# Turning gathered token rows by DMA transposes instead of TensorE for three pairs of tiles, and moving two small steps a place later

## The chip, the cores and the metric

One Trainium2 chip, of which one core runs the program. The metric is the device time of one execution in microseconds, lower is better.

## The reference

A gated linear attention recurrence, whose output rows are the tokens of a mixture of experts with two experts for each token.

```python
B, H, S, D = (4, 8, 768, 48)
for t in range(S):
    state = alpha[:, :, t, :, None] * state + einsum('bhd,bhe->bhde', k[:, :, t], v[:, :, t])
    y[:, :, t] = einsum('bhd,bhde->bhe', q[:, :, t], state)
x = y.transpose(0, 2, 1, 3).reshape(3072, 384)
...
logits = x @ w_gate                                  # 8 experts
noisy_logits = logits + log1p(exp(x @ w_noise)) * noise
top2, top2_w = the two largest of each row, and their softmax
for e in range(8):
    h = maximum(x[mask] @ w1[e], 0.0)                # w1: 384 x 1024
    out[mask] += top2_w[mask, k, None] * (h @ w2[e]) # w2: 1024 x 384
```

All of it is in float32. (`log1p(exp(z))` is computed on the chip as an exponential and then a logarithm with 1 added to its input.)

## The kernel before

The kernel has two stages. The order of the instructions on each engine is written out by hand, and each engine works through its own in that order.

**The recurrence** goes over 24 chunks of 128 tokens, n = 0 to 23; six chunks are a batch and also a unit (u = 0 to 3) of the router. A chunk is a list of pieces in a fixed order: 0 loads, 1 keys, 2 inverses, 3 alphas, 4 turn_y, 5 turn_k, 6 scaled, 7 queries, 8 block, 9 output, 10 no_more, 11 state, 12 scores, 13 masked, 14 products. Within these, a piece works for a chunk further on or further back: `scores` and `masked` are those of chunk n + 1, `turn_y` is that of n - 1. TensorE (PE) turns the inputs (`tp`, L343), multiplies scores (L423), turns the keys (L450), forms the output (y, L491 and L252) and turns it into rows with the router's logits (L275); VectorE (DVE) runs two scans over the chunk (L371, L383), scales the queries (L411) and masks the scores (L443); ScalarE (ACT) copies from PSUM.

The router's work for a unit is a generator, `routing`, of nine or ten steps: the exponential (L719), the logarithm (L687), the first sums, the search for the two largest of two columns (L733, L734), of two more, then of the last two together with the exponential of the gates (L751), the counts on DVE (L757 to L781), the rank on PE (L786, L787), the table entries, and for unit 1 a check of the lists. The exponential and the logarithm need different tables of ACT, so a table load stands ahead of each switch. For units 0 and 1, `ROUTE` says behind which piece of which chunk a step goes: a pair (c, place) is chunk c + 5 of unit 0 and chunk c + 11 of unit 1. For units 2 and 3, the steps have planned times in the second stage.

**The experts** work on 24 pairs of tiles of 128 tokens, i = 0 to 23, counted from 0 here as in the code, so the fourth to the seventh pair are i = 3 to 6. Pairs 0 to 7 take the first 256 tokens of each expert, each with new weights; from pair 8 on, two pairs share the weights of an expert. The matrix products follow a scheme that saves multiplications with sums of blocks on DVE. Each step of a pair has a planned time 20 i + t. All steps of all pairs, of some small tiles and of the router's units 2 and 3 are sorted by their planned times, and that is the order of their instructions on each engine. (20 units of this plan take about 19.6 us in the first pairs.) For unit 3 the exponential and the logarithm are planned at 49.8.

What brings the rows of x of a pair to PE:
- `load_tab` reads 256 entries of the table (SP's queue for the pairs 0, 1 and 5 to 8, POOL's for the others), `find_rows` computes row numbers on DVE, and `gather` fetches the rows from DRAM into `x_in` by two indirect DMAs on POOL (L988). A row lies there as two planes of 16 bits, the low and the high halves of its 384 words.
- By TensorE (pairs 0 to 6): `joined_rows` copies the planes on ACT into whole words in `x_whole` (L286, two copies of 128 x 768 halves); `turn_x` turns 3 blocks of 128 x 128 for each of the two tiles on PE (L1191, the product into a PSUM bank of `tp`); `turned_x` copies each of the two banks into `xts` on ACT (L1195). For the pairs 3 to 6 (`in_turn`) the joins are planned at -13.9, the turns at -7.9 and -3.25 and the copies at -7.0 and -2.4.
- By the DMA (from pair 7 on): `turn_x` issues two DMA transposes of 128 x 768 halves on SP's queue (L1187), from `x_in` into `x_turned`, which is the same memory as `x_whole`; `turned_x` puts the halves together with two copies on ACT (L1198). Pair 7 has the transposes planned at -20.5, and the copies at -10.0 and -8.5.

`scaled` (L1352) is ACT's copy of a bank of the second product times the gate, `added` and `added_to_both` (L1356, L1360) add a bank to it on DVE, `relu` is L1342, and L1323, L1331 and L1338 are the products. Bank A (`o_ps`) is written by a product, scaled by ACT, and written again.

`out_of_range` tests in two parts whether a fast form of the recurrence was in range: part 0 is five small steps on DVE, planned at 117.4, part 1 a product with ones on PE (L525) and two small steps on DVE (L526, L527).

Of the kernel before, what the change touches and what calls it, by code (L numbers as in the profile page):

```python
# [19 lines left out]
def kernel(  # L20
# [35 lines left out]
    E, _, F = moe_w1.shape  # L56
# [228 lines left out]
    def whole(to, planes, copy):  # L285
        copy(out=to.bitcast(U16).rearrange("p (c w) -> p w c", w=2), in_=planes.rearrange("p (w c) -> p w c", w=2))  # L286
# [5 lines left out]
    def fast_gla(on):  # L292
# [210 lines left out]

        ROUTE = (((1, 9), (2, 8), (2, 13), (3, 4), (3, 11), (4, 8), (4, 10), (5, 4), (5, 7)), ((1, 9), (1, 12), (2, 4), (2, 8), (2, 11), (3, 8), (3, 10), (4, 4), (4, 7), (4, 12)))
        routes = [routing(u, on) for u in range(NU)]

        def route(n, place):
            for u in range(2):  # L510
                for _ in range(ROUTE[u].count((n - (u + 1) * UC + 1, place))):
                    next(routes[u], None)
# [579 lines left out]
    order_of = list(range(E)) + [E - 1 - g for g in range(E) for b in range(2)]  # L1092
    rounds = [0] * E + [1, 2] * E
    PLANNED = E + 2 * AFTER_GROUP[0]
    DEEP, BY_DMA = E - 1, E - 1
    is_new = [i < E or (i % 2 == 0 and order_of[i] != order_of[i - 1]) for i in range(NPAIR)]
    assert len(order_of) == NPAIR

# [1 line left out]
    def pairs(on):  # L1100
# [75 lines left out]
                get_x(x_in[:, s], wheres[i][:, s, 0:1], 2 if i < E else NU)  # L1176

        def joined_rows(i):
            if i >= BY_DMA:
                return  # L1180
            for s in range(2):
                whole(x_whole[:, s], x_in[:, s], nc.scalar.copy if i else nc.vector.tensor_copy)

        def turn_x(i, some=range(2)):
            for s in some:
                if i >= BY_DMA:
                    nc.sync.dma_start_transpose(out=x_turned[:, s].rearrange("p w a t -> p (w a) t"), in_=x_in[:, s])  # L1187
                    continue
                x_ps = bank["x", s] = on["tp"].tile([C, KO, C], F32, tag="tp", name="x_ps")
                for a in range(KO):  # L1190
                    nc.tensor.transpose(x_ps[:, a, :], x_whole[:, s, ds(a * C, C)], ident)  # L1191

        def turned_x(i, part):
            if i < BY_DMA:
                nc.scalar.copy(xts[i % 2][:, part], bank["x", part])  # L1195
                return
            halves = xts[i % 2].rearrange("p s a t -> p (s a t)").bitcast(U16).rearrange("p (s x w) -> p w s x", s=2, w=2)
            nc.scalar.copy(halves[:, part], x_turned[:, :, part].rearrange("p s a t -> p s (a t)"))  # L1198

        def rows_x(i):  # L1200
            return lambda a, t: xts[i % 2][:, t, a, :]
# [178 lines left out]
        T = 20.0  # L1380
        FIRST_BEHIND = 2
# [105 lines left out]
        def steps(i):  # L1487
            w = lambda f, a: w1_(i, f, a)
            v = lambda f, d: w2_(i, f, d)
            x = rows_x(i)  # L1490
            apart = i < FIRST_BEHIND
            full = i < E
            early = {0: EARLY_0, 1: EARLY_1, FIRST_BEHIND + 1: {"tab": T * i - 40.0, "find": T * i - 33.0, "gather": T * i - 32.5}, E - 1: {"tab": T * E - 57.5, "find": T * E - 52.3, "gather": T * E - 52.2},
                     E: {"tab": T * E - 33.0, "find": T * E - 25.0, "gather": T * E - 24.8, "turn": T * E - 21.8, "turned": T * E - 9.5, "joined": T * E - 8.0}}.get(i, {})
            at = lambda name, t: early.get(name, T * i + t) - T * i
            in_turn = FIRST_BEHIND < i < BY_DMA
            if full and i >= BY_DMA:
                gets = {"tab": -32.0, "find": -27.0, "gather": -26.0, "join": -22.0, "turn": -20.5, "turned": -10.0, "joined": -8.5, "sum_x": -0.5, "sum_xs": 0.3}
            elif in_turn:
                gets = {"tab": -32.0, "find": -27.0, "gather": -26.0, "join": -13.9, "turned": -7.0, "joined": -2.4, "sum_x": -0.5, "sum_xs": 0.3}  # L1500
            elif full:
                gets = {"tab": -32.0, "find": -27.0, "gather": -26.0, "join": -15.0, "turn": -11.9, "turned": -11.0,
                        "joined": -11.0, "sum_x": -7.9 if apart else -10.38, "sum_xs": -7.9 if apart else 0.3}
            else:
                gets = {"tab": -50.5, "find": -32.5 if i % 2 else -39.4, "gather": -29.5, "join": -31.0, "turn": -23.5, "turned": -12.4, "joined": -11.2,
                        "sum_x": -6.4, "sum_xs": 0.3}
            when = lambda name: at(name, gets[name])
            turns = [(-7.9, lambda: turn_x(i, (0,))), (-3.25, lambda: turn_x(i, (1,)))] if in_turn else [(when("turn"), lambda: turn_x(i))]
            w1_at = (-20.0, -17.0, -14.0 if i >= DEEP else -3.5) if i > FIRST_BEHIND else [at("w1", -29.5) + part * every.get(("w1", i), 3.0) for part in range(KO)]
            w2_at = (5.5, 8.2, 10.9, 13.6) if i > FIRST_BEHIND else [at("w2", -19.8) + part * every.get(("w2", i), 3.0) for part in range(FO // 2)]  # L1510
            loads = [(t, lambda w=w, part=part: load_part(w, i, part)) for w, ts in (("w1", w1_at), ("w2", w2_at)) for part, t in enumerate(ts)]
            s_at = (-16.5, -15.8, -7.4, -7.5) if apart else (-12.0, -11.3, -9.5, -8.8)
            t_at = (-5.2, -2.5, 0.1, 4.4) if i == 0 else (20.4, 24.6, 27.5, 24.7) if i > E else (14.5, 24.0, 27.5, 25.0)
            last = i == NPAIR - 1
            second_layer = (parted if i == 0 else last_ending if last else mixed)(i, v)
            return [(T * i + t, go) for t, go in loads] + [(T * i + t, go) for t, go in (
                (when("tab"), lambda: load_tab(i)), (when("find"), lambda: find_rows(i)), (when("gather"), lambda: gather(i)),
                (when("join"), lambda: joined_rows(i)), *turns,
                (when("turned"), lambda: turned_x(i, 0)), (when("joined"), lambda: turned_x(i, 1)),
                *([(t, lambda k=k: sum_x_deep(i, k)) for k, t in enumerate((-7.5, -7.4, -5.2, 4.5, 8.6) if i <= E else (-9.0, -8.0, -5.2, 4.5, 8.6))] if i >= DEEP else  # L1520
                  [(when("sum_x"), lambda: sum_x(i, True)), (when("sum_xs"), lambda: sum_x(i, False))]),
                *([(t, lambda k=k: sum_w1_deep(i, k)) for k, t in enumerate((-9.5, -7.0, -0.9, 0.05, 2.5, 6.0, 8.0, 10.9))] if i >= DEEP else
                  [(at(f"s{k}", t), lambda k=k: sum_w1(i, k)) for k, t in enumerate(s_at)]),
                *[(at(f"t{k}", t), lambda k=k: sum_w2(i, k)) for k, t in enumerate(t_at)],
                *(deeper(i, x) if i >= DEEP else (alone if apart else between)(i, w, x)), *second_layer)]
# [159 lines left out]
    with ExitStack() as es:  # L1685
# [5 lines left out]
        pair_steps, clear_pairs, T, latest = pairs(on)  # L1691
# [3 lines left out]
        def beside():  # L1695

            at = (-0.95, 4.75, 3.66, 6.15, 6.9, 28.5)
            left = [(at[0], lambda: put_y(LAST - 2)), (at[1], lambda: output(LAST)), (at[2], lambda: turn_y(LAST - 1)),
                    (at[3], lambda: turn_y(LAST)), (at[4], lambda: put_y(LAST - 1)), (at[5], lambda: put_y(LAST)),
                    (5 * T + 17.4, lambda: out_of_range(0)), (5 * T + 18.7, lambda: out_of_range(1))]  # L1700
            r1, r2, r3 = (6.2, 12.2, 15.2)
            when = lambda *steps: [d * T + t for d, t in steps]
            left += [(t, lambda: route_on(2)) for t in when(*((0, 17.4), (0, 17.4), (0, 18.7), (1, r1), (2, 3.5), (2, r1), (2, 9.7), (2, r2), (2, r3)))]
            left += [(t, lambda: route_on(3)) for t in when(*((2, 9.8), (2, 9.8), (3, r1), (3, r1), (3, r2), (3, r3), (4, r1), (4, r2), (4, r3)))]
            left += [(t, lambda: route_on(3)) for t in when(*[(8, 10.7), (9, 1.6), (9, 8.7), (9, 10.7), (10, 10.7), (10, 12.2), (10, 13.2), (11, 1.6)])]
            puts = when((2, 17.3), (2, 18.6), *[(3, t) for t in (3.9, 5.2, 10.1, 11.4, 12.7, 17.3, 18.6)],
                        (4, 3.9), (4, 5.2), (4, 11.4), (4, 17.3), (4, 18.6), *[(5, t) for t in (3.9, 5.2, 10.1, 11.4, 12.7, 17.3, 18.6)],
                        (6, 2.6), (6, 3.9), (6, 5.2))
            left += [(t, lambda: put_some(1, latest["sum"])) for t in puts]
            assert len(puts) == 4 * UC  # L1710
            return left
# [156 lines left out]
```

## Time and profile before

| | |
|---|---|
| time before, median of 3 runs | 632.79 us (632.18 to 632.89) |
| the profiled execution | 634.14 us, span 632.5 us |
| TensorE (PE), busy | 613.7 us |
| VectorE (DVE) | 512.2 us |
| ScalarE (ACT) | 330.4 us |
| GpSimd (POOL) | 323.2 us |
| mean granted TensorE clock | 0.995 |

The profile is of one execution, and its times are microseconds from the first instruction on. The span reaches from the first instruction to the last; what lies around it belongs to the execution's own time. "Busy" leaves out waits, and a busy PE is not PE at its peak, since matmuls are pipelined. A wait is put down to the engine and instruction that ended it.

### The profile page before, as it was taken

The numbers are of one execution on the slowest core, as the hardware profiler recorded it, in microseconds if no ns is written. First come the engines' busy times: TensorE is split into PE (matmuls) and PEld (weight loads), VectorE is DVE, ScalarE is ACT, GpSimd is POOL, SyncE is SP. The second block draws the span as 40 slices with busy tenths as digits, with TensorE's granted clock in tenths as the row PEclk, the third lists the DMA queues.
The fourth block names the chain that finished last, engine by engine and source line by source line (L and its number), as shares of the span: only waits on it lengthen the run. The fifth ranks groups of instructions, "written<-read, shape, count | busy, mean of one in ns | idle before, by whom it ended". The sixth has DMA issues, their size and how long they took to land.

```text
span 632.5 us, 14445 instructions
## 1 busy us (share of the span) xinstructions
PE 613.7 (97%) x5326; PEld 589.3 (93%) x5326; DVE 512.2 (81%) x1175; ACT 330.4 (52%) x664; POOL 323.2 (51%) x362
## 2 busy tenths in 40 slices
PE   8999999999999999999999999999999999999993
PEld 5899989988999999999999999999999999989893
DVE  8788998878759877578999999787987879878671
ACT  5778777675555453342555454545545545454340
POOL 7353277854051877775545465532655427443353
PEclk9999999999999999999999999999999999999997
DMA  9999999984862666785746776866869578775223
GB/s 144 167 199 214 219 201 170 226 160 112 264 194 100 205 199 182 205 248 98 176 103 134 176 242 135 225 149 154 260 161 234 123 181 226 178 213 134 63 40 53
DMA packets 178288, 108.56 MB, mean 172 GB/s; under 512 B 142600, under 2 KB 167667, under 8 KB 178209
## 3 DMA queue, kind: packets, MB, share of 16 engines
q1 hardware_dynamic: 137040, 33.59, 31.1%
q10 hardware_dynamic: 25840, 53.48, 27.7%
q0 software_dynamic: 15328, 20.47, 14.5%
q8 instruction: 44, 0.72, 0.5%
q14 instruction: 36, 0.29, 0.1%
HBM read 85.85 MB, written 24.22 MB: 174 GB/s over the span
## 4 chain that ended last, share of the span: by engine, by line
PE 75%; DVE 12%; issue 3%; DMA 3%; POOL 2%; ACT 2%; SPq 0%; POOLq 0%; DVEq 0%; ACTq 0%
PE h_ps L1338 14%; PE sc L1331 13%; PE o_ps L1338 11%; PE sc L1323 7%; PE c_ps L1331 6%; PE tp L343 5%; PE sc L423 4%; PE y L252 4%; PE h_ps L275 3%; PE y L491 3%; DVE wt L1204 1%; PE o_ps L465 1%; PE tp L450 1%; PE c_ps L1323 1%; DVE h L1207 1%
## 5 line engine op out<-in xcount | busy, mean ns | idle before, releaser
L972 POOL DMA_INDIRECT out_dram<-o,where x46 | 48.5, 1055 | 150.4 <-DVE o L1356 70.4
L1342 ACT ACTIVATE h<-h 128x512 f32<-128x512 f32 x89 | 55.2, 628 | 84.4 <-DVE h L1204 51.6
L988 POOL DMA_INDIRECT x_in<-x_rows,where x48 | 59.6, 1242 | 53.9 <-DVE where L1172 29.5
L980 POOL DMA_INDIRECT out_dram<-o,where x44 | 74.7, 1697 | 13.4 <-issue 13.4
L1338 PE MATMUL o_ps<-wt,hx 128*128 128x192 f32 x384 | 70.7, 327 | 0.0
L1338 PEld LDWEIGHTS o_ps<-wt,hx 128*128 128x128 f32 x384 | 61.5, 190 | 1.8 <-issue 1.8
L172 POOL DMA_INDIRECT table<-entry,place_u x48 | 53.1, 1106 | 13.9 <-issue 10.9
L1331 PE MATMUL sc<-yT,ws 128*128 128x128 f32 x408 | 56.5, 275 | 0.0
L1331 PEld LDWEIGHTS sc<-yT,ws 128*128 128x128 f32 x408 | 53.5, 191 | 0.0
L401 POOL TENSOR_TENSOR k_P<-k_P,over 128x512 f32<-128x512 f32 (+1 forms) x24 | 27.7, 1155 | 44.6 <-DVE over L383 31.5
L343 PE MATMUL tp<-ident,ins 128*128 128x128 f32 x288 | 42.0, 280 | 2.2 <-ACT k_P L393 0.7
L1352 ACT ACTIVATE o<-h_ps,tab 128x192 f32<-128x192 f32 x46 | 19.3, 420 | 40.9 <-PE h_ps L1338 33.7
L343 PEld LDWEIGHTS tp<-ident,ins 128*128 128x128 f32 x288 | 31.8, 142 | 7.2 <-ACT k_P L393 1.1
L443 DVE COPY_PREDICATED shared<-upto,sc 128x512 f32<-128x512 uint32 x47 | 31.9, 732 | 6.9 <-PE sc L423 6.4
L1338 PE MATMUL h_ps<-w,hx 128*128 128x192 f32 x192 | 35.6, 327 | 0.3 <-issue 0.3
L1338 PE MATMUL h_ps<-wt,h 128*128 128x192 f32 x192 | 35.3, 327 | 0.3 <-DVE wt L1204 0.3
L1338 PE MATMUL o_ps<-w,h 128*128 128x192 f32 x192 | 35.3, 327 | 0.2 <-DVE o L1360 0.2
L1338 PE MATMUL h_ps<-wt,hx 128*128 128x192 f32 x192 | 35.2, 326 | 0.0
L1338 PE MATMUL h_ps<-w,h 128*128 128x192 f32 x192 | 35.1, 326 | 0.0
L1198 ACT COPY xt<-x_turned 128x768 uint16<-128x768 uint16 x34 | 33.6, 1053 | 0.8 <-DMA x_turned<-x_in 0.8
L1338 PEld LDWEIGHTS h_ps<-w,hx 128*128 128x128 f32 x192 | 31.7, 190 | 0.7 <-issue 0.7
L1338 PEld LDWEIGHTS h_ps<-w,h 128*128 128x128 f32 x192 | 31.8, 190 | 0.0
(322 smaller groups left out, 1642.1 us busy)
## 6 DMA issues: line engine op xcount, KB each, us to landing
w<-in_moe_w_dram ACTq DMA_DIRECT2D x42, 512.0 KB
w<-in_moe_w_dram ACTq DMA_DIRECT2D x56, 384.0 KB
ins<-in_alpha_dram SPq DMA_DIRECT2D x24, 192.0 KB
ins<-in_k_dram SPq DMA_DIRECT2D x24, 192.0 KB
ins<-in_q_dram SPq DMA_DIRECT2D x24, 192.0 KB
vt<-in_v_dram SPq DMA_DIRECT2D x24, 192.0 KB
x_rows<-y_sb SPq DMA_DIRECT2D x24, 192.0 KB
ins<-in_moe_w_dram ACTq DMA_DIRECT2D x9, 512.0 KB
```

The lines of the kernel that those rows point to most:

```text
L172: put = nc.gpsimd.indirect_dma_start(out=table, out_offset=bass.IndirectOffsetOnAxis(ap=place, axis=0), in_=entry, in_offset=None, bounds_ ...
L343: nc.tensor.transpose(tp[:, j, :], src[:, 2 * j:2 * j + 2, :], ident)
L401: (nc.vector if n == NT - 1 else nc.gpsimd).tensor_tensor(c["k"][:, at], c["k"][:, at], over[:, at, 1:CB], op=ALU.mult)
L443: nc.vector.copy_predicated(MTs[n % 2][:, i], mask_upto, sc)
L972: put = nc.gpsimd.indirect_dma_start(out=out, out_offset=bass.IndirectOffsetOnAxis(ap=at, axis=0), in_=rows, in_offset=None, bounds_check= ...
L980: add = nc.gpsimd.indirect_dma_start(out=out, out_offset=bass.IndirectOffsetOnAxis(ap=at, axis=0), in_=rows, in_offset=None, bounds_check= ...
L988: nc.gpsimd.indirect_dma_start(out=rows, out_offset=None, in_=x_rows[0:units * UT, :], in_offset=bass.IndirectOffsetOnAxis(ap=at, axis=0), ...
L1198: nc.scalar.copy(halves[:, part], x_turned[:, :, part].rearrange("p s a t -> p s (a t)"))
L1323: nc.tensor.matmul(bank[name][:, f, :], W[:, ds(f * C, C)], X, start=new and f == 0, stop=True, skip_group_check=True)
L1331: nc.tensor.matmul(bank[name][:, 2 * h + f, :], W[h][:, ds(f * C, C)], X[h], start=new and not h and not f, stop=True, skip_group_check=True)
L1338: nc.tensor.matmul(bank[name], H[:, f, :], W[:, f, :], start=new and f == 0, stop=True, skip_group_check=True)
L1342: nc.scalar.activation(t, t if src is None else src, AF.Relu)
```

## The change

The pairs that PE turns are now 0, 1, 2 and 6, so the pairs 3, 4 and 5 take the way by the DMA, with its planned times: transposes at -20.5, copies at -10.0 and -8.5 (that is 39.5, 50.0 and 51.5 for pair 3), and no join.

In `ROUTE`, unit 1's second step, the logarithm, moves from (1, 12) to (2, 8); its third to fifth steps (the first sums and two searches) move from (2, 4), (2, 8) and (2, 11) to (2, 11), (2, 13) and (3, 4); the others stay.

The second part of the range test moves from a planned time of 118.7 to 127.0.

```diff
-        ROUTE = (((1, 9), (2, 8), (2, 13), (3, 4), (3, 11), (4, 8), (4, 10), (5, 4), (5, 7)), ((1, 9), (1, 12), (2, 4), (2, 8), (2, 11), (3, 8), (3, 10), (4, 4), (4, 7), (4, 12)))
+        ROUTE = (((1, 9), (2, 8), (2, 13), (3, 4), (3, 11), (4, 8), (4, 10), (5, 4), (5, 7)), ((1, 9), (2, 8), (2, 11), (2, 13), (3, 4), (3, 8), (3, 10), (4, 4), (4, 7), (4, 12)))
...
-    DEEP, BY_DMA = E - 1, E - 1
+    DEEP, BY_TENSOR = E - 1, (0, 1, 2, E - 2)
...
         def joined_rows(i):
-            if i >= BY_DMA:
+            if i not in BY_TENSOR:
                 return
...
         def turn_x(i, some=range(2)):
             for s in some:
-                if i >= BY_DMA:
+                if i not in BY_TENSOR:
                     nc.sync.dma_start_transpose(out=x_turned[:, s].rearrange("p w a t -> p (w a) t"), in_=x_in[:, s])
                     continue
...
         def turned_x(i, part):
-            if i < BY_DMA:
+            if i in BY_TENSOR:
                 nc.scalar.copy(xts[i % 2][:, part], bank["x", part])
                 return
...
-            in_turn = FIRST_BEHIND < i < BY_DMA
-            if full and i >= BY_DMA:
+            in_turn = FIRST_BEHIND < i and i in BY_TENSOR
+            if full and i not in BY_TENSOR:
                 gets = {"tab": -32.0, "find": -27.0, "gather": -26.0, "join": -22.0, "turn": -20.5, "turned": -10.0, "joined": -8.5, "sum_x": -0.5, "sum_xs": 0.3}
...
-                    (5 * T + 17.4, lambda: out_of_range(0)), (5 * T + 18.7, lambda: out_of_range(1))]
+                    (5 * T + 17.4, lambda: out_of_range(0)), (6 * T + 7.0, lambda: out_of_range(1))]
```

## Rows read from the trace of the kernel before

**Rows 1.** The page, part 1: busy time, share of the span, instructions.
```profile
PE 613.7 (97%) x5326; PEld 589.3 (93%) x5326; DVE 512.2 (81%) x1175; ACT 330.4 (52%) x664; POOL 323.2 (51%) x362
```

**Rows 2.** PE's waits: who waited for whom, us in total, times, longest.
```profile
PE tp L450 <- ACT noisy L687: 1.4, 1, 1.4
```

**Rows 3.** Timeline near the range test: start, us, engine, line, operation, [idle before, releaser].
```profile
268.59 0.69 DVE L1207 TENSOR_TENSOR h<-c_ps,m 128x512 f32<-128x512 f32 x1 [5.03 <-PE x_ps L1191]
269.33 1.05 PE L1323 MATMUL sc<-xt,w 128*128 128x128 f32 x8
...
271.22 0.38 PE L525 MATMUL count<-out_of,ones 128*128 128x3 f32 x2 [0.84 <-DVE out_of L536]
```

**Rows 4.** The chain that ended last, near pair 3: start, us, what.
```profile
203.93 0.61 DVE h L1207
...
204.58 2.05 PE sc L1323 x16
...
207.94 0.33 PE x_ps L1191 x3
...
209.56 1.78 PE sc L1323 x16
```

**Rows 5.** Timeline, unit 1's logarithm, ACT and PE's weight loads.
```profile
92.45 1.28 ACT L687 ACT_TABLE_LOAD   x1
...
94.71 0.42 PEld L450 LDWEIGHTS tp<-ident,k_P 128*128 128x128 f32 x4 [1.53 <-issue]
```

**Rows 6.** Timeline, chunks 13 and 14, and two rows of chunk 20.
```profile
98.10 1.16 PE L423 MATMUL sc<-q_P,k_P 48*128 48x128 f32 x16
...
99.15 0.16 DVE L733 MAX8 top<-noisy 128x8 f32<-128x8 f32 x1
...
99.84 1.34 DVE L443 COPY_PREDICATED shared<-upto,sc 128x512 f32<-128x512 uint32 x2
...
105.17 0.17 DVE L745 TENSOR_TENSOR entry<-top 128x12 f32<-128x12 f32 x1
105.37 0.23 ACT L751 ACTIVATE entry<-entry 128x12 f32<-128x12 f32 x1 [0.84 <-DVE entry L745]
...
107.41 0.44 PE L787 MATMUL h_ps<-past,ones 128*128 128x48 f32 x2
...
142.78 1.16 PE L423 MATMUL sc<-q_P,k_P 48*128 48x128 f32 x16
...
143.97 1.36 DVE L443 COPY_PREDICATED shared<-upto,sc 128x512 f32<-128x512 uint32 x2 [0.62 <-PE sc L423]
```

**Rows 7.** Timeline, pairs 8 and 9: gather, DMA transposes, ACT's copies behind them.
```profile
291.29 1.05 POOL L988 DMA_INDIRECT x_in<-x_rows,where  x1 [6.08 <-DVE where L1172]
...
294.46 2.94 SPq L1187 DMA_TRANSPOSE x_turned<-x_in  x2
...
302.05 1.07 ACT L1198 COPY xt<-x_turned 128x768 uint16<-128x768 uint16 x1 [0.78 <-DMA x_turned<-x_in]
...
316.46 1.97 ACT L1198 COPY xt<-x_turned 128x768 uint16<-128x768 uint16 x2
```

**Rows 8.** Timeline ahead of pair 4: its gather, ACT, and PE's use of bank A.
```profile
205.71 1.79 POOL L988 DMA_INDIRECT x_in<-x_rows,where  x1 [6.18 <-ACT o L1352]
...
220.16 0.42 ACT L1352 ACTIVATE o<-h_ps,tab 128x192 f32<-128x192 f32 x1 [1.66 <-PE h_ps L1338]
...
223.44 0.63 ACT L1342 ACTIVATE h<-h 128x512 f32<-128x512 f32 x1 [2.86 <-DMA w<-in_moe_w_dram]
...
226.06 1.47 PE L1338 MATMUL o_ps<-wt,hx 128*128 128x192 f32 x8
```

**Rows 9.** Timeline of ACT ahead of pair 3.
```profile
202.76 0.24 ACT L719 ACTIVATE noisy<-lg 128x48 f32<-128x48 f32 x1 [2.60 <-DVE lg L713]
203.02 1.28 ACT L687 ACT_TABLE_LOAD   x1
...
205.09 0.41 ACT L1352 ACTIVATE o<-o_ps,tab 128x192 f32<-128x192 f32 x1
```

## The prediction

> **What bounds the kernel now.** The page's first part comes first: PE is busy for 97% of the span, no other engine for more than 81% [rows 1], so a change pays only where it takes work or a wait from PE's queue, and costs where it adds a wait to it. PE's list of waits is then nearly empty. What stands out in it is 1.4 us for the logarithm's instruction (L687) [rows 2], and in the timeline 0.84 us for the range test (L525) [rows 3]. The edit moves these two. The chain of waits shows that between 195 and 204.5 us it is not PE but VectorE, without a pause, that sets the time (PE goes on at 204.58, when DVE's h is done) [rows 4]; elsewhere near the change the chain is PE alone. The timeline gives the rest.
>
> **The logarithm, a place later.** Now: the table load of unit 1's logarithm stands on ACT from 92.45 on, ahead of the copy of k that frees a PSUM buffer, and PE's turn of k waits: its weights are loaded 1.53 us late, at 94.71 [rows 5]. At its new place (chunk 13, behind block) ACT has no copy that PE needs soon: unit 0's logarithm stands at just that place, and PE's list of waits has L687 once among the four units' [rows 2]. So PE comes some 1.5 us earlier to chunk 14. There it meets the next wait. Behind the logarithm, three more steps slide: the first two of the search for the maxima go behind `masked` of chunk 13 and the next two to chunk 14's place 4, but the last two with the gates' exponential stay at (3, 8). That exponential is queued on ACT ahead of the copy yT, and waits for DVE already now (0.84 us at 105.37); PE's matmul of rank, L787, comes at 107.41 straight behind DVE's counts, which follow the exponential [rows 6].
>
> When will DVE be there? Scores of chunk 13 now start at 98.10; 1.5 earlier is 96.56. `masked` can follow them 1.19 us later, as it does where DVE is free (142.78, 143.97): 97.75. From `masked` to the subtraction that the exponential waits for, DVE now takes 99.84 to 105.17 = 5.33 us; two more searches, of two columns each, come into that stretch, 0.69 us each (one runs from 99.15 to `masked` at 99.84): 6.71, so 104.46, 0.7 us earlier than now and not 1.5 [rows 6]. Whatever hangs on it (exponential, yT, counts, rank) gains 0.7, and PE with it. I take **-0.7**, between 0 (DVE slower by another 0.7) and -1.5 (PE's whole wait).
>
> **The range test, a place later.** The counting matmul waits 0.84 us for DVE; PE's eight matmuls before it start at 269.33 and take 0.89 us (half of the sixteen at 209.56 [rows 4]), so PE stands from 270.22 to 271.22 [rows 3]: upper bound -1.0. The matmul's own time moves along; at its new place its input is 6 us old. DVE's two small steps move with it, past pair 5's hx, which stays ahead of them, and delay only a sum of w2 that PE wants 8 us later. But the test is late only because DVE stood still for 5.03 us before 268.59, a wait in no other pair, put down to a matmul long begun [rows 3]. The profiled execution, 634.14 us (span 632.5 and 1.64 around it), is 1.35 longer than the median of 632.79; if the standstill belongs to it alone, nothing is gained. **-0.5**, the middle of 0 and -1.0.
>
> **The turns.** Per pair, PE loses 6 transposes in two groups of 0.33 us [rows 4]: 0.66, for three pairs 1.97 us. ACT loses two joins and two PSUM copies and gets two copies of x_turned, 1.97 us together [rows 7]; SP gets two DMA transposes per pair, and the gathers stay.
>
> *Pairs 4 and 5.* The DMA's price is read from pair 8: gather at 291.29, first transpose issued 3.2 us behind it at 294.46, and ACT's copy, waiting for it, starts at 302.05: 7.6 us from issue [rows 7]. Pair 4's gather is issued at 205.71 [rows 8], so the issue is near 209 and landing near 217. ACT comes to the copies behind the scaling at 220.16, thus 220.58; both copies are over at 222.6, and the relu behind them waits for other things until 223.44 [rows 8]. So they lie in ACT's idle time. The reserve is larger: PE needs the scaling behind that relu (1.0 us for both) at 226.06 [rows 8], so landing may slip to about 223. On SP, the transposes of pairs 4 and 5 now stand ahead of the small table loads of pairs 5 and 6 and make them wait for the gathers; what reads those, the search for rows on DVE, is planned 13.5 us behind the transposes, and that hides it. Pair 5 repeats all this some 20 us later. PE's four groups are saved whole: **-1.3**; bounds 0 (the copies late by as much) and -1.3.
>
> *Pair 3.* Its first group (planned 52.1, just ahead of this place) goes for nothing: PE waits for DVE at 204.58 in any case. Its second (207.94) is worth 0.33 [rows 4]. But the new copies have planned times 50.0 and 51.5, and unit 3's exponential and logarithm have 49.8. ACT, in order, waits 2.60 us for DVE's lg, takes the table load at 203.02, and is free 0.26 us behind it, at 204.56 [rows 9]. Today the relu and then the scaling of bank A (205.09, over at 205.50) follow. With the change the two copies come first, 1.97 us, and the scaling ends at 207.47. PE writes bank A again in o_ps, which it reaches at 204.58 + 1.78 (sixteen matmuls, as at 209.56) = 206.36 [rows 4]: it has to wait until 207.5. Behind it on ACT are two relus, needed by PE some 3 us later. Price +1.1, less 0.33: **+0.7**. Bounds: -0.66 (copies placed where ACT waits, both groups saved) and +1.5 (both copies whole, 1.97, with little slack).
>
> Sum: -0.7 - 0.5 - 1.3 + 0.7 = -1.8 us, on the median **631.0**.
>
> A rule that speaks against the change: the Trainium skill, "VectorE: DVE Perf Modes", sections "The three transpose paths" and "Rules for kernel authors", would have a 128x128 transpose done by TensorE where PSUM will do, and gives the DMA 1309 ns for one of 2-byte elements against 390 ns. A pair has twelve such, 15.7 us by that figure (an estimate); pair 8's twelve took 7.6 us, half of it [rows 7], so the trace disagrees with the figure. By it the copies of pairs 4 and 5 would each come nearly 2 us behind their reserve, and the sum would be about +2.
>
> **Rivals.**
> 1. *All waits just vanish* (0.2): DVE makes up its 0.7 us in chunk 14, the standstill is in every execution, and pair 3's copies find room. -1.5 - 1.0 - 1.3 - 0.33 = -4.1: 628.7. For it: in the chunks DVE still waits for PE here and there [rows 6]. Against it: the order on ACT [rows 9].
> 2. *Gains given back* (0.2): the exponential of chunk 14 takes the whole of what the logarithm gave, the standstill was the profile's, and pair 3 costs its 0.7: -1.3 + 0.7 = -0.6: 632.2, no change that can be told.
> 3. *The transposes land late* (0.12), the other side. First-round pairs load new weights each, 3 MB a pair, and pair 8's stretch fewer; a landing twice as long (15.2 us) comes at 224.2 for pair 4 and 1.2 us past the reserve, the same for pair 5, and with pair 3 the change is -1.8 + 2.5 = +0.7: 633.5. It decides from 14 us between issue and landing on; each us more costs one in each of two pairs. Against it: the 6 us of reserve, and that of the 17 pairs turned so now the list of waits has one that waited, 0.78 us [rows 7].
> The Trainium skill's 15.7 us, above, is this rival's case.
>
> **How the numbers follow.** The forecast has 0.48, with its own range 630.0 to 632.0. Below 0.2% (1.3 us) a measurement of this kernel can't tell a change from none: 631.5 and 634.1 are the limits. Of the forecast's chance three quarters lie under 631.5 (0.36), and all of rival 1's (0.2): faster 0.57, with a little of rival 2. Rival 2 and most of rival 3 stay within 0.2%; slower needs late landings by some 2 us each and keeps 0.08; same 0.35. The range runs from rival 1 to rival 3 with all but its latest landings: 628.6 to 633.5.
>
> **What would show it.** In the changed trace: no wait of PE for L687, but a gap ahead of rank or the rows' matmul of chunk 14 of about 0.7 us; count without a wait; no x_ps on PE for pairs 3 to 5; on ACT near 203 the copies L1198 between the logarithm and the relu, and a wait of o_ps for ACT of about 1 us; in pairs 4 and 5 copies without a wait for x_turned, and pair starts 0.7 us nearer together. I am wrong if DVE, not PE, takes over between 210 and 260 us, if ACT waits there for the DMA, or if 5 us of standstill turn up elsewhere.

## The result, and the profile after

The change is slower: 637.89 us, the median of 16 runs (630.89 to 642.59), beside 632.10 for the kernel before (16 runs, 631.19 to 633.73). The ratio on record, here and below, is not one of the two medians and leaves out executions far above the fastest, three of the change's here: 1.0074, 95% interval 1.0057 to 1.0092. In a later comparison it was 635.33 beside 631.45 (below). The spread is part of the result: 12 us between runs of one program, where the kernel before has 2.5. The profiled execution of the change is one of its long ones (642.41 us, span 640.7).

TensorE's list of waits after, beside [rows 2] (us in total, times, longest):
```profile
PE sc L1323 <- DVE h L1207: 8.8, 2, 8.3
PE sc L1331 <- ACT m L1469: 1.4, 1, 1.4
...
PE o_ps L1338 <- ACT o L1352: 1.2, 2, 0.6
```
The logarithm (L687) and the range test (L525) are gone from it, as the change meant. One wait of 8.3 us has come. Where these stand, in the timeline of PE (start, us, engine, line, operation, idle before and its releaser):
```profile
105.44 1.15 PE L275 MATMUL h_ps<-to_rows,yT 128*128 128x112 f32 x8 [0.51 <-ACT yT L494]
...
202.43 2.05 PE L1323 MATMUL sc<-xs,w 128*128 128x128 f32 x16 [0.45 <-DVE h L1207]
...
205.10 1.57 PE L1338 MATMUL o_ps<-wt,hx 128*128 128x192 f32 x8 [0.63 <-ACT o L1352]
...
250.22 3.75 PE L1323 MATMUL sc<-xs,w 128*128 128x128 f32 x16 [8.34 <-DVE h L1207]
...
311.86 0.71 PE L1331 MATMUL sc<-xt,q_P 128*128 128x128 f32 x4 [1.37 <-ACT m L1469]
```
105.44 is the small gap that was forecast at chunk 14, 0.51 us. 202.43 and 205.10 are pair 3's, forecast as one of 1.1 us. 250.22 was not forecast: TensorE stands for 8.34 us ahead of pair 5. 311.86 is at pair 8, which had its turns by the DMA before as well; ScalarE waits 3.35 us for turned rows there. (Pairs are counted from 0 here as in the code; the expectations below call pairs 3, 4, 5 and 7 the fourth, fifth, sixth and eighth.) The same stretch on SP's queue, on ScalarE and on VectorE:
```profile
228.13 3.02 SPq L1187 DMA_TRANSPOSE x_turned<-x_in  x2
```
```profile
229.19 0.35 ACTq L1148 DMA_DIRECT2D w<-in_moe_w_dram  x1
...
230.10 0.33 ACTq L1148 DMA_DIRECT2D w<-in_moe_w_dram  x1
...
246.45 1.05 ACT L1198 COPY xt<-x_turned 128x768 uint16<-128x768 uint16 x1 [5.00 <-DMA x_turned<-x_in]
```
```profile
246.87 0.69 DVE L1207 TENSOR_TENSOR ws<-w 128x512 f32<-128x512 f32 x1 [8.66 <-DMA w<-in_moe_w_dram]
```
SP issues the two turns of pair 5 at 228.13. ScalarE issues pair 5's first two blocks of w1 at 229.19 and 230.10 (by their order in the queue). The turned rows are there for ScalarE only at 246.45, 18.3 us after the issue, and the weights for VectorE's first sum only at 246.87, the second block having landed 16.65 us after its issue. The chain of waits (start, us, what) goes through the weights:
```profile
230.10 16.65 DMA w<-in_moe_w_dram
...
250.22 3.75 PE sc L1323 x16
```
So two transfers are late: ScalarE stands 5.00 us for the one, VectorE 8.66 us for the other. Now the DMA itself, by queue, in 2 us of that stretch, 236 to 238 (packets, MB, time of the packets as a share of 16 engines); q1 is SP's queue with the turns, q10 ScalarE's with the weights:
```profile
q1 hardware_dynamic: 270, 0.07, 84.0%
q10 hardware_dynamic: 58, 0.21, 57.7%
```
The kernel before in 232 to 234, where no packet of q1 ran beside q10's, and those were of like size (4 KB; 3.6 KB above):
```profile
q10 hardware_dynamic: 112, 0.45, 70.7%
```
And ten microseconds of both, 232 to 242, the kernel before and then the change:
```profile
q10 hardware_dynamic: 966, 2.04, 69.1%
```
```profile
q10 hardware_dynamic: 216, 0.78, 59.0%
q1 hardware_dynamic: 985, 0.23, 47.9%
```
The DMA as a whole was not idle there before: the windows of the kernel before (busy time by engine, granted clock, DMA share, GB/s) have
```profile
228.00:230.00 2.00, 2.00 (x18) 2.00 (x17) 0.65 (x2) 1.08 (x2) 0.69 (x2) 1.00 0.64 174
...
234.00:236.00 2.00, 2.00 (x18) 2.00 (x18) 1.97 (x4) 1.17 (x3) 1.50 (x2) 1.00 0.97 272
```
And four microseconds of the changed kernel in which the turns have nearly no company (pair 3's, 194 to 198):
```profile
q1 hardware_dynamic: 800, 0.20, 22.1%
q10 hardware_dynamic: 48, 0.13, 8.4%
```
The share times 16 engines times the window, over the packets, is the time of one: a turn's packet takes 18 ns in the last window (0.221 x 64 us / 800) and 100 ns beside the weights; a packet of the weights takes 202 ns before and 318 ns after. (The two shares add to more than 1, so packets of the two queues are under way at the same time.) Both queues slow down, and together they move half: 1.01 MB in the ten microseconds, where the weights alone moved 2.04.

### The profile page after: what moved, and what is told of

It reads as the page before. It is cut to its first block, busy times and chain, and to the rows that moved or that the text cites. A ratio compares the mean times of both kernels' runs of the same rounds, so it can differ in the third digit from the quotient of the medians.

```text
span 640.7 us, 14415 instructions
## 1 busy us (share of the span) xinstructions
PE 613.4 (96%) x5308; PEld 589.4 (92%) x5308; DVE 512.0 (80%) x1175; ACT 327.8 (51%) x658; POOL 324.0 (51%) x362
## 4 chain that ended last, share of the span: by engine, by line
PE 68%; DVE 14%; DMA 8%; issue 4%; ACT 3%; POOL 1%; SPq 0%; ACTq 0%; POOLq 0%; DVEq 0%
PE h_ps L1338 13%; PE sc L1331 13%; PE o_ps L1338 10%; PE c_ps L1331 6%; PE sc L1323 5%; PE tp L343 4%; PE sc L423 3%; PE y L252 3%; PE h_ps L275 3%; DMA w<-in_moe_w_dram 3%; PE y L491 2%; DMA x_in<-x_rows,where 1%; DMA out_dram<-o,where 1%; DVE wt L1204 1%; DMA x_turned<-x_in 1%
## 5 line engine op out<-in xcount | busy, mean ns | idle before, releaser
L980 POOL DMA_INDIRECT out_dram<-o,where x44 | 73.5, 1671 | 13.4 <-issue 13.4
L1198 ACT COPY xt<-x_turned 128x768 uint16<-128x768 uint16 x40 | 39.4, 1052 | 8.3 <-DMA x_turned<-x_in 8.3
```

The costliest lines, as they stand in the source:

```text
L980: add = nc.gpsimd.indirect_dma_start(out=out, out_offset=bass.IndirectOffsetOnAxis(ap=at, axis=0), in_=rows, in_offset=None, bounds_check= ...
```

## Experiments

All ratios are against the kernel before, timed beside it on the same chip.

**The two moves alone.** BY_TENSOR covers pairs 0 to 6 again:
```
-    DEEP, BY_TENSOR = E - 1, (0, 1, 2, E - 2)
+    DEEP, BY_TENSOR = E - 1, tuple(range(E - 1))
```


> The two moves alone (second unit's logarithm and range test later), with the rows of the fourth to sixth pair turned by TensorE as before. Theory A, the loss lies in the DMA turns (in the profile after, TensorE stands 8.3 us before the sixth pair, until weights issued 16.6 us before have landed, and the turned rows issued at 228 land at 246): the moves give about what the sum gave them, -1.2 us, so 630.5 to 631.5 us beside 632.1 before. Theory C, the moves themselves collide (the range test or the logarithm at its new place): slower than 633.


629.96 beside 629.65 us, ratio 1.0004 (0.9996 to 1.0013): nothing lost (theory C falls), but nothing gained.

**The turns alone.** The routes and the range test as before, BY_TENSOR as in the change.


> The DMA turns of the fourth to sixth pair alone, with logarithm and range test at their old places. Theory A: all of the loss and its spread, 637 to 640 us, with single runs from 632 to 643. Theory C: near 631.5 us, the -0.6 that the sum gave the turns.


635.34 us, 1.0106 (1.0076 to 1.0135), runs from 631.38 to 640.65: the loss and its spread are the turns'.

**Turns that nobody reads.** Pairs 3 to 5 are turned by TensorE, and besides by the DMA into the tile prev:
```
+        def nobody_reads(i):
+            if 3 <= i <= 5:
...
+                    nc.sync.dma_start_transpose(out=spare[:, s], in_=x_in[:, s])
+            if i == 12:
+                nc.gpsimd.memset(prev, 0.0)
...
+                (-20.5, lambda: nobody_reads(i)),
```


> The moves as in the change; the rows of the fourth to sixth pair are turned by TensorE as before, and the DMA makes the same turns at the same places besides, into a tile that nobody reads (cleared again at the thirteenth pair). Theory A1, the turns and the weights slow one another down in the DMA, so that weights come late: most of the loss stays, 635 to 640 us, with a stand of TensorE and VectorE until weights have landed. Theory A2, the loss is ScalarE standing in order at the copies of rows that land late, with weights issued behind them: nobody waits for the turns here, so 630.5 to 632 us.


631.00 us, 1.0052 (1.0021 to 1.0082). Seven of its 12 runs lie between 629.46 and 631.03, as A2 said, five between 633.61 and 638.30, as A1 said. Its profile is one of the five (633.61); VectorE and then TensorE in it:
```profile
241.31 0.69 DVE L1215 TENSOR_TENSOR ws<-w 128x512 f32<-128x512 f32 x1 [2.68 <-DMA w<-in_moe_w_dram]
```
```profile
244.66 3.49 PE L1331 MATMUL sc<-xs,w 128*128 128x128 f32 x16 [1.83 <-DVE h L1215]
```
Weights come late although no engine waits for a turned row. So the contention is real, and it strikes in fewer runs than in the change. What is missing from the whole loss (1.0106 for the turns alone) may be what ScalarE's standing at the copies adds, as A2 has it; no run settles that.

**Pair 5 by TensorE, 3 and 4 by the DMA.**
```
+    DEEP, BY_TENSOR = E - 1, (0, 1, 2, E - 3, E - 2)
```


> The change, but the sixth pair's rows turned by TensorE as before; fourth and fifth by the DMA. If the loss is the one place that the profile shows (the sixth pair's turns, 18 us from issue to landing, where the fourth's and fifth's are done some 4 and 3 us before they are read): 630.5 to 632 us. If any pair's turns can meet the weights that badly, from run to run another: two thirds of the loss, 634 to 637 us.


629.85 us, 1.0002 (0.9993 to 1.0011). Without pair 5's turns the loss is gone.

**The kernel before, profiled again.**


> The kernel before once more, for a profile from the same chip as the variants. The two moves alone came out level with it there (629.96 beside 629.65 us) although the sum gave them -1.2. If the waits that they were to remove (the logarithm's 1.4 us and the range test's 0.8 us of TensorE) are there again, and the span is still level with that of the moves alone, the moves give the time back later; if the waits are missing here, there was nothing to gain.


One run, 629.35 us; its chip is not that of the two moves alone. PE in it, and POOL's product that PE's turn of k waits for in each chunk:
```profile
94.93 0.63 PE L450 MATMUL tp<-ident,k_P 128*128 128x128 f32 x4 [1.37 <-ACT k_P L393]
...
127.76 0.62 PE L465 MATMUL o_ps<-vt,k_end 128*64 128x48 f32 x16
...
140.22 0.62 PE L465 MATMUL o_ps<-vt,k_end 128*64 128x48 f32 x16
```
```profile
135.98 1.20 POOL L401 TENSOR_TENSOR k_P<-k_P,over 128x512 f32<-128x512 f32 x1
```
The same of the two moves alone:
```profile
105.52 1.15 PE L275 MATMUL h_ps<-to_rows,yT 128*128 128x112 f32 x8 [0.52 <-ACT yT L494]
...
127.02 0.62 PE L465 MATMUL o_ps<-vt,k_end 128*64 128x48 f32 x16
...
137.57 0.66 PE L450 MATMUL tp<-ident,k_P 128*128 128x128 f32 x4 [0.35 <-POOL k_P L401]
...
140.41 0.62 PE L465 MATMUL o_ps<-vt,k_end 128*64 128x48 f32 x16
```
```profile
124.88 1.83 POOL L172 DMA_INDIRECT table<-entry,place_u  x1 [0.17 <-issue]
127.01 1.21 POOL L172 DMA_INDIRECT table<-entry,place_u  x1 [0.30 <-issue]
128.52 0.98 POOL L172 DMA_INDIRECT table<-entry,place_u  x1 [0.30 <-DVE S L470]
...
136.32 1.19 POOL L401 TENSOR_TENSOR k_P<-k_P,over 128x512 f32<-128x512 f32 x1
```
The logarithm's wait is there again (1.37 us at 94.93, named after the copy behind it), and with the move 0.52 us at 105.52 takes its place: TensorE is 0.74 us earlier at 127 (127.76, 127.02). But POOL is not. Its queue holds the same scatters into the table in both; three of them, from 124.88 on, take 4.0 us here (1.83, 1.21, 0.98), and took 3.0 before (1.00, 0.97, 1.02). So its product for the chunk at 137 starts at 136.32 instead of 135.98; TensorE waits 0.35 us for it, and at 140 it is 0.19 us later than before (140.22, 140.41). The turns alone, without the move and on the chip of the two moves, have 127.65 and 140.11. The move's gain lives for 35 us.

POOL does not take it in all. There are 15 profiles of versions with the move and five without it. At 122 TensorE is ahead in all 15 (o_ps at 121.51 to 122.26, without the move 122.31 to 122.63). Six of them then have this wait for POOL; the other nine, the change's own two among them, have a wait of 0.2 to 0.3 us near 123 instead, and four of these one of 0.4 to 0.5 near 128. (Three of the five without the move have such waits too.) At 146 the ranges overlap: 145.25 to 146.33 with the move, 145.47 to 147.59 without. Why the scatters take longer is open.

The range test's 0.84 us is not in this second profile of before at all; in two other versions with the test at its old place it was 0.27 and 0.24 us.

**Without the accumulating transfers.** add_tile is left out for pair 2:
```
-            if i:
+            if i and i != 2:
```


> The change, with the two accumulating transfers of the third pair's second rows left out (they start some 1 us after and 7 us after the sixth pair's turns are issued), so the output lacks that addition. Theory A1a, the turns crawl because accumulating writes hold the DMA up beside them: the sixth pair's turns land within 10 us and the time falls to 631 to 632. Theory A1b, it is turns against weights: still 635 to 640.


634.81 us, 1.0058 (1.0037 to 1.0080): not those (A1b).

**Without pair 5's w1.**
```
-            if is_new[i]:
+            if is_new[i] and (w, i) != ("w1", 5):
```
(and now[w, 5] is pair 4's).


> The change, with the sixth pair's three first-layer weight transfers left out (the fifth pair's are used once more); two of them are issued within 2 us of the sixth pair's turns. Theory A1b, turns against weights: the turned rows land before ScalarE comes to them and TensorE has no weights to wait for, 630 to 632 us. Theory A1a: the turns still take over 14 us, ScalarE stands some 5 us for them, and half of the loss or more stays, 633 to 637.


629.30 us, 0.9997 (0.9989 to 1.0006). The loss is gone, and the turns, issued at 228.45, are through with the window that ends at 234 (no packet of q1 in the next 2 us):
```profile
q1 hardware_dynamic: 2104, 0.40, 66.4%
```
5.5 us instead of 18.3. By the Trainium skill, "VectorE: DVE Perf Modes", section "The three transpose paths", twelve would take 15.7 us (the prediction's estimate, from 1309 ns for one); the trace agrees neither here nor in the change. The twelve are the same in both; what runs beside them is not.

**Later copies.** In short:
```
+  "turn": -16.5, "turned": -7.0, "joined": -2.4   (pairs 3 to 5)
```


> The change, with the DMA turns of the fourth to sixth pair issued 4 units later (behind the two weight transfers of the pair's own first layer) and their copies 3 and 6.1 units later. If what costs is that the first-layer weights, needed within 8 us, share the DMA with the turns, the weights get ahead and little of the loss stays: 630 to 633 us. If turns beside any weights cost that much, 635 us or more, with ScalarE or VectorE standing for the turned rows instead.


635.69 us, 1.0077 (1.0047 to 1.0106). The turns did not in fact move: SP waits for nothing but the gathered rows and issued them at 228.02. So this tried the copies' places alone, and VectorE and TensorE still stand for weights:
```profile
243.44 0.69 DVE L1207 TENSOR_TENSOR ws<-w 128x512 f32<-128x512 f32 x1 [5.46 <-DMA w<-in_moe_w_dram]
```
```profile
246.78 3.78 PE L1323 MATMUL sc<-xs,w 128*128 128x128 f32 x16 [4.92 <-DVE h L1207]
```

**Pairs 3 and 4, copies later, moves undone.**


> The turns of the fourth and fifth pair alone by the DMA, their two copies 3 and 6.1 units later (behind the scaling of bank A that they held up: TensorE's 0.63 us at 205 in the change's profile), logarithm and range test at their old places. By the sum: two pairs without six transposes each, 0.65 us each, less the new 0.45 us before the fifth pair: 628.5 to 629.2 us beside 629.5. If what is taken from TensorE there comes back as other waits, as it did with the moves (0.85 us gained at 106, 0.9 lost between 130 and 140): 629.3 to 630.2.


631.39 beside 631.70 us, 1.0007 (0.9989 to 1.0025): level. The wait of o_ps is gone from its timeline, and the time is none the shorter for it. Two of its 12 runs lie at 636, although pair 5's turns are by TensorE here; the highest of 31 runs of the kernel before is 633.97.

**The turns behind the weights, in ScalarE's queue.** With the later copies:
```
-                    nc.sync.dma_start_transpose(out=x_turned...
+                    (nc.scalar if i < DEEP else nc.sync).dma_start_transpose(out=x_turned...
+  "turn": -16.9, "turned": -7.0, "joined": -2.4   (pairs 3 to 5)
```


> The change with the later copies, but the fourth to sixth pair's turns issued by ScalarE, in the same DMA queue as the weights and behind the pair's first two weight transfers, so that no turn runs beside an earlier weight transfer's start. Theory B1, the crawl comes of turns and weights from two queues sharing the DMA engines packet by packet: the weights land in time, 629 to 631 us. Theory B2, any turn in that stretch overloads the DMA, whatever the order (with the weights the DMA was at 0.8 of its time before): 634 to 638, as with the turns in a queue of their own (635.7).


630.34 us, 0.9972 (0.9961 to 0.9982). ScalarE at pair 5, and the DMA in the same 2 us as above:
```profile
230.43 0.34 ACTq L1148 DMA_DIRECT2D w<-in_moe_w_dram  x1
230.88 2.83 ACTq L1187 DMA_TRANSPOSE x_turned<-x_in  x2
...
242.47 1.04 ACT L1198 COPY xt<-x_turned 128x768 uint16<-128x768 uint16 x1
```
```profile
q10 hardware_dynamic: 1211, 0.53, 97.9%
```
The turns are issued 2.75 us later than in the change and copied at 242.47 without a wait; VectorE has none for weights. 0.53 MB go through q10 in the 2 us, and 2.09 in the ten from 232 to 242. Theory B2 falls. Of B1 it is shown that the loss needs the two queues, not how they share the DMA.

**Pair 5's w1 behind the turns, in SP's queue.**
```
-                by = nc.sync if i == 0 else nc.scalar
+                by = nc.sync if i == 0 or (w, i) == ("w1", 5) else nc.scalar
```


> The change, with the sixth pair's first-layer weights issued in the turns' queue, behind the turns. Theory B1: the turns run nearly by themselves, as without these weights (5 to 6 us), and the weights, 4 us behind them, land about when they are needed: 630 to 633 us. Theory B2: 635 to 640.


630.72 us, 0.9989 (0.9973 to 1.0004): level with before. The other order in one queue mends it as well, with the turns issued at 228.79, so it is not their later issue alone that did it above.

**Pair 5 alone by the DMA.**


> The change with the sixth pair's turns alone by the DMA (fourth and fifth by TensorE). If the sixth pair's place alone makes the collision: all of the loss, 634 to 638. If it takes the two pairs before it as well (turned rows, gathers and weights that shift with them): 630 to 632.


632.48 beside 631.70 us, 1.0007 (0.9994 to 1.0020). Neither forecast: its profile shows TensorE standing 2.39 us at 244.70 for sums of late weights, but the median hardly rises. What pairs 3 and 4 add to the collision is not settled.

**Both versions on one chip, and the queue by itself.**


> The change once more, beside the versions of this call on one chip: 635 to 639 us, spread over 8 us or more from run to run.

> The version with the turns of the fourth to sixth pair behind the weights in ScalarE's queue, their copies later, once more: between 0.1% and 0.4% under the kernel before if the gain of 0.28% holds on another chip; level if that chip's kernel before was merely slow.

> The same, with the copies at the change's places: only queue and place of the turns differ from the change. Theory B1 (order in the DMA): 630 to 632 us, at most 1 us over the version with later copies, by the fourth pair's copies on the scaling of bank A (0.6 us at 205 in the change's profile) and by ScalarE waiting for turns that land 4 us later. If the later copies were what mended it: 634 or more.


Beside 631.45 us before: the change 635.33, 1.0069 (1.0044 to 1.0095); the queue with later copies 631.61, 1.0010 (0.9983 to 1.0036); the queue with the change's copy places 631.08, 0.9997 (0.9977 to 1.0018). So the queue alone takes the loss away, and the gain of 0.28% did not come again.

The change's profile here is of its shortest execution (632.62 us). TensorE does not stand at pair 5 in it, and the turns, issued at 229.23, are there 10.2 us later. ScalarE's copy, then the DMA in 230 to 232 and in 234 to 236:
```profile
239.43 1.07 ACT L1198 COPY xt<-x_turned 128x768 uint16<-128x768 uint16 x1 [0.40 <-DMA x_turned<-x_in]
```
```profile
q1 hardware_dynamic: 800, 0.20, 60.6%
...
q10 hardware_dynamic: 14, 0.05, 19.1%
```
```profile
q10 hardware_dynamic: 165, 0.58, 93.7%
q1 hardware_dynamic: 84, 0.02, 4.7%
```
The same program with the same two queues: here the turns go through nearly alone (24 ns a packet), then the weights nearly alone, and 2.17 MB go through both from 232 to 242. In the long execution both queues move in every 2 us of that stretch, and 1.01 MB go through. So these two profiles tie the loss to the two running mixed, which one queue keeps them from. What decides in an execution with two queues is open.

Both mended versions still have single runs far up, to 637.28 with later copies and 636.35 without. The profile of the queue alone is one such (635.36 us), and TensorE does not stand at pair 5 in it; the place is pair 8's, which already had its turns from SP before. ScalarE and PE there:
```profile
300.89 1.04 ACT L1198 COPY xt<-x_turned 128x768 uint16<-128x768 uint16 x1 [3.85 <-DMA x_turned<-x_in]
```
```profile
302.43 0.71 PE L1331 MATMUL sc<-xt,q_P 128*128 128x128 f32 x4 [1.87 <-ACT m L1469]
...
304.14 2.55 PE L1338 MATMUL o_ps<-wt,hx 128*128 128x192 f32 x8 [0.56 <-ACT o L1352]
```
In the kernel before that wait for x_turned was 0.78 us [rows 7], and TensorE did not stand.

**All later turns in ScalarE's queue too.**


> The version with later copies, and the turns of the eighth and all later pairs in ScalarE's queue too, the eighth's behind its first weights. If turns in a queue of their own cost the later pairs something too (in the kernel before, ScalarE waited 0.8 us once for turned rows, and the spread of its times on two chips is 2.5 to 3.4 us): another 0.5 to 2 us less, with a narrower spread. If not: level with the version before it, or slower by what ScalarE then waits for gathered rows before it can issue a turn (1 us or more in a pair, 16 pairs).


638.59 us, 1.0102 (1.0079 to 1.0126). ScalarE has to wait for gathered rows before it can issue a turn, and all behind it waits too, at pair 8:
```profile
292.55 2.62 ACTq L1187 DMA_TRANSPOSE x_turned<-x_in  x2
295.22 0.63 ACT L1342 ACTIVATE h<-h 128x512 f32<-128x512 f32 x1 [9.89 <-issue]
```
ScalarE stands 9.89 us, and TensorE 3.4 us for ScalarE behind it. In order with the weights is good only where the rows are there already.

**Pair 7 by TensorE**, in the kernel before and in the version with ScalarE's queue (join at -16.0, turns at -13.4 and -11.0).


> The kernel before, with the eighth pair's rows turned by TensorE as well (so no turn by the DMA beside first-round weights). If the eighth pair's turns collide with weights too: the slow single runs go (spread 1 us instead of 2.5 to 3.4) and the median falls by 0.5 to 1.5 us. If not: 0.65 us or so slower, for six transposes more on TensorE and two joins more on ScalarE.

> The version with the fourth to sixth pair's turns behind the weights in ScalarE's queue and the later copies, and the eighth pair's rows turned by TensorE. If the runs of 4 to 7 us above the best come from the eighth pair: median 629 to 630 and a spread of 2 us. If they come from the turns of the ninth pair and later, or still from the sixth: the spread stays 6 to 8 us.


633.10 beside 631.76 us, 1.0018 (1.0008 to 1.0027), spread 1.8; and 630.88, 0.9983 (0.9973 to 0.9994), spread 3.5. By itself a loss, of more than the 0.65 us expected; with the queue the only version here whose interval lies under the kernel before in all that was timed of it, by 0.17%, and less narrow than hoped. It was timed once, and so was the gain of 0.28% that did not come again.

## Why the prediction was wrong

**The step that failed is pairs 4 and 5**, "bounds 0 (the copies late by as much) and -1.3". For pair 5 it should have had a loss of several us as its bound. Two things were wrong in it. The DMA's price, 7.6 us, was read at pair 8, whose stretch loads fewer weights, and the reserve of 14 us between issue and landing was held against it; in the stretch where the turns were to run they took 18.3 us in the long execution that was profiled, and 10.2 in a short one. Rival 3 had this half of it, with 0.12 of the chance. What neither it nor the rest had is the other half: the turns slow the weights that share the stretch, and TensorE stood for those (8.34 us), not for the turned rows. Taking the weights away (629.30) or putting both in one queue (631.08) ends the loss; moving the copies (635.69) does not; unread turns bring part of it. Of the signs that the prediction's last sentence named, ScalarE waiting for the DMA came (5.00 us), and so did a standstill (8.66 us of VectorE). VectorE did not take over by its own work: it, too, waited for weights.

**Pair 4 and pair 3** came out right in sum: +0.7 and -0.65 were forecast, and with these two turned by the DMA the time is that of the moves alone, 629.85 and 629.96 us, each to within some 0.6 us. The two terms are not shown by that: with pair 3's price taken away by later copies the time did not fall under that of the kernel before, so the agreement may be luck. Pair 3's place was right too, its size less: bank A costs 0.63 us instead of 1.1. Half of the difference is a reading, since the sixteen matmuls at 204.58 take 2.05 us in [rows 4] and the text took 1.78 from others. The 0.45 us for VectorE just before it stand where the first group's transposes were, whose saving the text had not counted.

**The logarithm** gave what was worked out where it was worked out: a new gap of 0.52 us where about 0.7 stood in the text, and TensorE 0.85 us earlier (1.37 less 0.52). The term failed after that: the sum carried the gain to the end, and waits 15 to 35 us further on, which were not looked at, took it back (POOL's product in six of 15 profiles). This is rival 2 by another mechanism.

**The range test** gave nothing that the time shows, instead of -0.5. The doubt was in the text, that the wait belonged to the one profiled execution; the second profile of before has neither the wait nor the standstill ahead of it. Its bound of -1.0 was a little high as well: the wait itself is 0.84 us [rows 3]. The same list of waits has 1.1 us of TensorE's o_ps (L465) for ScalarE, more than that, and the prediction passed over it; the second profile does not have it either.

**The sum**, then: logarithm 0, range test 0, pairs 3 and 4 0, pair 5 some +4 to +6 us in the median, from one comparison to the next, and up to +10 in a run.

**Open** is what decides from run to run whether the two queues mix, what pairs 3 and 4 add for pair 5, and where the long runs come from that the mended versions and the one with pairs 3 and 4 alone still have; one profile points at pair 8.

## What to carry to other kernels

Price a transfer in the stretch in which it will run, and ask what it does to the transfers that are there: the DMA's share was 0.64 to 0.97 already where 1600 small packets were added. Where transfers compete, put them in one queue in the order in which they are needed, but only if the queue's engine never has to wait for the data. And follow a gain on to the next wait that can take it back, which here was 15 to 35 us further on, at POOL in some profiles.

## What the runs showed of the hardware

Transfers of two queues can cost each other more than their sum. Pair 5's turns took 5.5 us without the weights beside them, and a 512 KB block of weights 4.3 us in the median of the kernel before. Together, in two queues, they took 18.3 and 16.65 us in the long execution. A turn's packet took 100 ns instead of 18 and a weight packet of like size 318 instead of 202, and from 232 to 242 us 1.01 MB went through; in one queue it was 2.09. In the short execution of the same program the two queues went one after the other, with 2.17 MB.

The granted clock makes a standstill of TensorE dearer than its length. In and after the 8.34 us of idling (241.88 to 250.22), in windows of the changed kernel (busy time by engine, granted clock, DMA share, GB/s):
```profile
244.00:246.00 2.00, 0.00 (x0) 0.00 (x0) 0.00 (x0) 0.00 (x0) 0.00 (x0) 1.00 1.01 254
...
248.00:250.00 2.00, 0.00 (x0) 0.00 (x0) 2.00 (x4) 0.41 (x1) 0.15 (x1) 0.50 0.63 216
250.00:252.00 2.00, 1.78 (x8) 1.78 (x9) 1.97 (x9) 1.57 (x3) 1.70 (x2) 0.50 0.35 84
```
The clock goes from 1.00 to 0.50 (2.4 to 1.2 GHz), and the sixteen matmuls that follow take 3.75 us, where the same sixteen behind the short wait at 202.43 took 2.05: 1.7 us on top of the 8.3. In the version with the queue alone, eight matmuls behind stands of 1.87 and 0.56 us took 2.55 us (granted clock 0.64 and 0.50 from 304 to 308), where eight behind the wait at 205.10 in the change took 1.57. The length of the stand alone does not tell: sixteen took 3.49 us behind 1.83 (unread turns, 0.75 and 0.50 from 244 to 248) and 2.05 behind 2.39 (pair 5 alone, 1.00).
